# Three of the first six loads issued from ScalarE's DMA queue, in a fused retention and feed-forward kernel

## The chip, the cores and the metric

The kernel runs on one core of one Trainium2 chip. The metric is device time in microseconds of one execution; lower is better. A profile is one further view of a single execution, so its span is compared with that execution's own time.

## The reference

Eight batches of eight heads, 576 positions of 64 values each, go through a retention layer: the scores are weighted with a decay that depends on the distance of the positions, and set to zero above the diagonal. The result, 4608 rows of 512, goes through two matrix products with a tanh Gelu between them.

```python
scores = scale * np.matmul(q, k.transpose(0, 1, 3, 2))
gamma = 1.0 - 2.0 ** (-5.0 - np.arange(H))
rel = pos[:, None] - pos[None, :]
Dmat = np.where(rel >= 0, gamma[:, None, None] ** rel[None, :, :], 0.0)
ret = np.matmul(scores * Dmat[None], v)
x = ret.transpose(0, 2, 1, 3).reshape(B * S, H * D)
h = x @ w_in        
g = 0.5 * h * (1.0 + np.tanh(c * (h + 0.044715 * h * h * h)))
out = g @ w_out
```

## The kernel before

**Work and tiles.** A batch of 576 positions is four chunks of 128 and a tail of 64. Loads fetch 256 positions of four heads at once (256 KB, a "ld" tile of 128 x 512 in 32-bit floats), named by batch, half s of the batch, half hh of the heads, and k, q or v. They are cast to 16 bits (cast_qk, cast_v; v is scaled by a table sc of decays), k and q are transposed on TensorE (tr, a bank of PSUM that ScalarE, VectorE or both, marked S2, copy into the tile T), scores are formed (score_mm, L385) and masked (mask_sc, L408). A running state carries what earlier chunks leave (state_mm, scan, put into the tile tbd); values and inter_mm form the output of the layer, and evac (L534) scales it by the table gx into the rows of x.

The feed-forward part works on a Block of 512 rows: sixteen products up (L583), each followed by a Gelu on ScalarE (L587), then seven products down (L726, called my, mz, mw, mv, mu, my2, mz2), which are a fast matrix multiplication with seven instead of eight products; VectorE and GpSimd form its sums (mix_sa, mix_sc, mix_d). In the last two blocks, the tails of all batches and batch 7, three pairs of the upward products are also done by a saving scheme: pair_a (L615) makes three PSUM banks pv, pw and py, pair_q (L627) lets ScalarE copy pv into cp and VectorE form four sums and differences in q, pair_b adds to py, pair_s adds py to two of the four, and pair_g is the Gelu.

**What sets the order.** Nothing is reordered by a scheduler: each engine runs its instructions in the order in which the program text calls them. The body is a list of units (upward and downward products) with a plan, a hand-written list of steps that follow each unit. The first ten units are empty; their steps are batch 0. Dummy matmuls on a tile of zeros (warm, L138, and pad, L147 and L149, counts in the table pads) keep TensorE running in the first 20 us. They are plain instructions, executed whether TensorE would have had to wait or not.

**Loads.** All loads are issued by SyncE, in the order of the calls of load_qkv and load_w (L188, L272). The first six are k, q for heads 0 to 3 of half 0 of batch 0, k for heads 4 to 7, v for heads 0 to 3, q for heads 4 to 7, and k for heads 0 to 3 of half 1. Eight completion semaphores go round for all loads, so the ninth load issued waits for the first to have landed, and so on; later loads also wait for their buffer.

**The start of ScalarE.** ScalarE begins with a dummy Exp (L88), by which the table of Exp is loaded while other constants are made; then four Exps that make gx (L121), one for sc (L122), one for gt (L124, used by scan), and a dummy Gelu (L125), which brings in the other table for the rest of the kernel. In the plan the first steps on batch 0 are: GpSimd zeroes tbd (L132) and casts q, then k; TensorE transposes q, which ScalarE copies, then k, of which ScalarE copies two quarters and VectorE the others; VectorE's copy waits for ScalarE's; then come the scores of the first four heads, VectorE's cast of the second k, the two masks, the cast of the second q, and so on.

Of the kernel before, what the change touches and what calls it, by code (L numbers as in the profile page):

```python
# [10 lines left out]
AF = mybir.ActivationFunctionType  # L11
ALU = mybir.AluOpType
F32 = mybir.dt.float32
# [6 lines left out]
def kernel(  # L20
# [22 lines left out]
    nc = tc.nc  # L43
# [4 lines left out]
    HP = H // 2  # L48
# [36 lines left out]

    wz = const.tile([128, 256], F16, name="wz")
    nc.vector.memset(wz, 0.0)
    nc.scalar.activation(out=p2[:, 3:4], in_=wz[:, 0:1], func=AF.Exp)  # L88

    lg = const.tile([128, 13], F32, name="lg")  # L90
    nc.vector.memset(lg[:, 12:13], math.log(scale))
# [7 lines left out]
    for hh in range(2):  # L99
# [4 lines left out]
            op=ALU.mult,  # L104
# [12 lines left out]


    gx = const.tile([128, HP, 2, 64], F32, name="gx")
    for p in range(HP):  # L120
        nc.scalar.activation(out=gx[:, p], in_=gi, func=AF.Exp, bias=lg[:, 12:13], scale=lg[:, 8 + p : 9 + p])  # L121
    nc.scalar.activation(out=sc, in_=ex, func=AF.Exp, bias=0.0, scale=-1.0)  # L122
    gt = const.tile([128, HP], F32, name="gt")
    nc.scalar.activation(out=gt, in_=lg[:, 8:12], func=AF.Exp, bias=0.0, scale=128.0)  # L124
    nc.scalar.activation(out=p2[:, 3:4], in_=wz[:, 0:1], func=AF.Gelu_apprx_tanh)  # L125


    tbd = [const.tile([128, NC, HP, 128], F16, name=f"tbd{i}") for i in range(2)]
# [15 lines left out]
    def pad(key, t, o=0):  # L144
        for _ in range(pads.pop(key, 0)):
            if t.dtype == F16:
                nc.tensor.transpose(t[:, 0:128], wz[:, 0:128], ident)  # L147
            else:
                nc.tensor.matmul(t[:, o : o + 128], wz[:, 0:128], wz[:, 0:128], start=(o == 0), stop=True, skip_group_check=True)  # L149

    NJ = NF // 2
# [33 lines left out]
    def load_qkv(b, s, hh, key, home=None):  # L185
        def one(home):
            t = ld(home)
            nc.sync.dma_start(  # L188
                out=t.rearrange("p (h e) -> p h e", h=4),
                in_=SRC[key][b, 4 * hh : 4 * hh + 4, 256 * s : 256 * s + 256, :].rearrange(  # L190
                    "h (p r) d -> p h (r d)", r=2
                ),
            )
            att[b][key, s, hh] = t

        todo.append((one, home))
        pump()
# [33 lines left out]
    def copy(eng, out, in_):  # L231
        (eng.copy if eng is nc.scalar else eng.tensor_copy)(out=out, in_=in_)  # L232
# [208 lines left out]
            )  # L441
            a["rett", hl] = x

    def state_mm(b, ss):
        a = att[b]
        us = [bank("us") for _ in range(2)]
        pad(("us", b, ss[0]), us[0])
        for n, s in enumerate(ss):
            a["U", s] = us, n
            for p in range(HP):  # L450
                hh, pp = divmod(p, 2)
                if p == 2:
                    pad(("us1", b, ss[0]), us[0], 256)
                o = 256 * n + 64 * p
                for r in range(2):
                    for c in range(2):
                        for hl in range(2):
                            w = slice(256 * r + 128 * pp + 64 * hl, 256 * r + 128 * pp + 64 * hl + 64)
                            nc.tensor.matmul(
                                us[c][half[hl], o : o + 64],  # L460
                                a["kq"][half[c], s, hh, 0, w],
                                a["v"][half[c], s, hh, w],
                                start=(r == 0), stop=(r == 1), skip_group_check=True,
                            )

    def scan(b, n):
        a = att[b]
        s, c = divmod(n, 2)
        us, i = a["U", s]
        uc = us[c][:, 256 * i : 256 * i + 256].rearrange("p (q d) -> p q d", d=64)  # L470
        if n > 0:
            t = sb.tile([128, HP, 64], F32, tag="vs", name="vs", bufs=1)
            nc.vector.tensor_tensor(out=t, in0=uc, in1=a["w", n - 1], op=ALU.add)
            uc = t
        w = sb.tile([128, HP, 64], F32, tag="ws", name="ws", bufs=2)
        nc.vector.tensor_tensor(out=w, in0=uc, in1=gt.unsqueeze(2).to_broadcast([128, HP, 64]), op=ALU.mult)  # L476
        a["w", n] = w

    def put(b, n, eng):
        w = att[b]["w", n]  # L480
        for hl in range(2):
            e = (A, V)[hl] if eng is S2 else eng
            copy(e, tbd[b % 2][half[hl], n, :, half[hl]], w[half[hl]])

    def values(b, s):
        a = att[b]
# [28 lines left out]
    def inter_mm(b, s, c):  # L515
        a = att[b]
        n = 2 * s + c
        if n > 0:
            pad(("in", b, n), a["U", (n - 1) // 2][0][0])
            for p in range(HP):  # L520
                hh, pp = divmod(p, 2)
                nc.tensor.matmul(  # L522
                    a["x", s][c][:, 128 * p : 128 * p + 128],
                    tbd[b % 2][:, n - 1, p, :],
                    a["T"][:, s, hh, 1, pp : pp + 3 : 2, half[c]],
                    start=False, stop=True, skip_group_check=True,
                )
# [32 lines left out]
    class Block:  # L560
# [54 lines left out]
        def pair_a(self, j):  # L615
            self.open()
            pv, pw, py = bank("pv"), bank("pw"), bank("py")
            self.pair[j] = pv, pw, py
            f, w = wf[j], w_in_sb[:, :, 256 * j : 256 * j + 256]
            mm = self.pair_mm  # L620
            mm(j, pv[:, 0:256], lambda c: f[:, 2 + c], lambda c: self.x_half(1, 2 + c), True)
            mm(j, pv[:, 256:512], lambda c: f[:, 4 + c], lambda c: self.x_half(0, c))
            mm(j, pw[:, 0:256], lambda c: f[:, c], lambda c: self.xf[2][:, c], True)
            mm(j, py[:, 0:256], lambda c: w[:, c, 0:128], lambda c: self.xf[0][:, c], True)
            mm(j, py[:, 256:512], lambda c: w[:, 2 + c, 128:256], lambda c: self.xf[1][:, c])

        def pair_q(self, j):  # L627
            pv, pw, py = self.pair[j]
            cp = sb.tile([128, 512], F32, tag="cv", name="cp", bufs=2)
            q = sb.tile([128, 1024], F32, tag="T", name="q", bufs=4)  # L630
            self.pair[j] = py, q
            nc.scalar.copy(out=cp, in_=pv)
            c2 = cp.rearrange("p (k c) -> p k c", k=2)
            q4 = q.rearrange("p (m c) -> p m c", m=4)
            nc.vector.tensor_tensor(
                out=q4[:, 0:4:3], in0=py.rearrange("p (k c) -> p k c", k=2), in1=c2, op=ALU.add
            )
            for m, k in ((2, 0), (1, 1)):
                nc.vector.tensor_tensor(out=q4[:, m], in0=pw[:, 0:256], in1=c2[:, k], op=ALU.subtract)

        def pair_b(self, j):
            py, q = self.pair[j]
# [3 lines left out]

        def pair_s(self, j):
            py, q = self.pair[j]
            q4 = q.rearrange("p (m c) -> p m c", m=4)
            nc.vector.tensor_tensor(  # L650
                out=q4[:, 1:3], in0=py.rearrange("p (k c) -> p k c", k=2), in1=q4[:, 1:3], op=ALU.add
            )

        def pair_g(self, j):
            q = self.pair.pop(j)[1]
            nc.scalar.activation(  # L656
                out=self.g(j).rearrange("p h (s c) -> p s h c", s=2),
                in_=q.rearrange("p (s h c) -> p s h c", s=2, h=2),
                func=AF.Gelu_apprx_tanh,
            )  # L660

# [43 lines left out]
        def product(self, m, js=range(NJ), us=(0, 1)):  # L705
# [14 lines left out]
                else:  # L720
                    self.bank[m] = bank(m)
            t = self.bank[m]
            for u in us:
                o = t[u] if isinstance(t, list) else t[:, 256 * u : 256 * u + 256]
                for j in js:
                    nc.tensor.matmul(  # L726
                        o,
                        lhs(j, slice(128 * u, 128 * u + 128)),
                        w_out_sb[:, j, w],
                        start=((u == 0 or isinstance(t, list)) and j == 0 and not more),  # L730
                        stop=(j == NJ - 1), skip_group_check=True,
                    )

        def quad(self, s, k):
            return self.ost[:, :, s, 256 * k : 256 * k + 256]
# [58 lines left out]
                in_=self.ost[:, us[0] : us[0] + n, s, 256 * k : 256 * k + 256],  # L794
            )

        def last(self):
            for m in MS[:-1]:
                self.down(m)
                for q in {"mv": [(0, 1)], "mu": [(1, 0)], "my2": [(1, 1)]}.get(m, ()):  # L800
                    self.store_quad(*q)
            for u in range(2):
                self.product("mz2", us=(u,))
                self.settle("mz2", u)
                self.store_quad(0, 0, (u,), (nc.scalar, nc.sync)[u])
# [26 lines left out]
    def add(plan, *entries):  # L832
        for u, step in entries:
            plan.setdefault(u, []).append(step)
        return plan

    tiles(0)
    E = loan("T", 8, 4)
    E3 = E[:]
# [7 lines left out]
    load_qkv(0, 0, 0, "v", None)  # L847
    load_qkv(0, 0, 1, "q", None)
    load_qkv(0, 1, 0, "k", None)
    load_qkv(0, 0, 1, "v", None)  # L850
    load_qkv(0, 1, 1, "k", None)
    load_qkv(0, 1, 0, "q", None)
# [633 lines left out]
```

## Time and profile before

| what | value |
|---|---|
| median of 4 runs | 298.05 us (297.25 to 298.76) |
| the profiled execution's own time | 297.66 us |
| its span in the profile | 295.9 us |
| granted TensorE clock, share of full | 0.999 |
| TensorE busy in the span | 289.1 us |
| VectorE, ScalarE, GpSimd busy | 230.7, 161.9, 120.9 us |
| bytes moved, mean rate | 52.48 MB, 177 GB/s |

Times in the trace count from the start of the span. A row of the timeline has the start, the duration from the first to the last of the merged instructions, the engine, the line, the operation, output and inputs, the count, and in brackets the idle time of the engine just before, with what ended it. SPq and ACTq are the queues of SyncE and ScalarE in which DMAs are issued: the duration there is that of the issuing, not of the transfer. A row of the view of waits has who waited for whom, the sum in us, how many times, and the longest.

### The profile page before, as it was taken

Reading aid. Unit: us, or ns where it says so; the run is one execution under the profiler, and the core shown is the slowest. Engines: PE = TensorE matmul, PEld = TensorE weight load, DVE = VectorE, ACT = ScalarE, POOL = GpSimd, SP = SyncE. Lnnn points to the kernel's source line nnn. Section 1 sums busy time; section 2 is a strip of 40 time slices with the busy share of each in tenths; the row PEclk is TensorE's granted clock in tenths of the full one; section 3 lists DMA queues with packets and bytes.
Section 4 is the critical chain, followed back from the end, with each engine's and each line's share of the span. In section 5 each row is a group of like instructions: output and inputs, shape, how many; then the busy total and the mean of one; then the engine's idle time right before and its main releaser. Section 6 shows DMA issues by size and latency. Waiting matters only on the chain.

```text
span 295.9 us, 8910 instructions
## 1 busy us (share of the span) xinstructions
PE 289.1 (98%) x3748; PEld 209.0 (71%) x3748; DVE 230.7 (78%) x434; ACT 161.9 (55%) x316; POOL 120.9 (41%) x142
## 2 busy tenths in 40 slices
PE   8989999999999999999999999999999999999995
PEld 6866478888885568656875587558755886786584
DVE  2796899999997997897568756877688198886753
ACT  7338789875546781665446544654345217606720
POOL 6734784375240441282073206369003005711760
PEclk9999999999999999999999999999999999999999
DMA  7999999869879999969983998481120003002204
GB/s 203 304 351 332 310 383 322 233 174 232 212 211 230 326 217 215 300 218 145 273 279 91 136 268 272 111 149 15 66 80 0 2 25 121 0 2 71 71 3 142
DMA packets 94712, 52.48 MB, mean 177 GB/s; under 512 B 38352, under 2 KB 88528, under 8 KB 94672
## 3 DMA queue, kind: packets, MB, share of 16 engines
q1 hardware_dynamic: 94336, 51.26, 65.1%
q10 hardware_dynamic: 336, 0.66, 0.8%
q8 instruction: 29, 0.48, 0.7%
q14 instruction: 11, 0.09, 0.1%
HBM read 36.70 MB, written 9.44 MB: 156 GB/s over the span
## 4 chain that ended last, share of the span: by engine, by line
PE 80%; DMA 9%; SPq 4%; DVE 2%; ACT 1%; POOL 1%; issue 1%; DVEq 0%
PE hp L583 28%; PE my L726 11%; PE mz L726 11%; PE mu L726 5%; PE mw L726 5%; PE mv L726 5%; DMA ld<-in_moe_w_in_dram 4%; PE hp L669 3%; SPq L188 3%; PE xs L495 2%; PE xs L522 2%; DMA ld<-in_moe_w_out_dram 2%; DMA loan<-in_moe_w_in_dram 2%; PE py L613 2%; PE st L395 1%; DMA loan<-in_moe_w_out_dram 1%
## 5 line engine op out<-in xcount | busy, mean ns | idle before, releaser
L583 PE MATMUL hp<-x,w_in_sb 128*128 128x512 f16 x408 | 93.9, 379 | 0.0
L587 ACT ACTIVATE gT<-hp 128x512 f16<-128x512 f32 x112 | 65.8, 598 | 42.2 <-PE hp L583 40.5
L583 PEld LDWEIGHTS <-w_in_sb 128*128 128x128 f16 x448 | 42.5, 98 | 44.4 <-issue 0.3
L726 PEld LDWEIGHTS <-gT 128*128 128x128 f16 x576 | 55.8, 98 | 8.0
L232 POOL CAST kq<-ld 128x512 f16<-128x512 f32 x31 | 21.7, 708 | 54.5 <-DMA ld<-in_k_dram 40.1
L408 DVE TENSOR_TENSOR ret<-st,cm 128x512 f16<-128x512 f32 x64 | 39.9, 679 | 4.0 <-PE st L395 3.7
L241 POOL TENSOR_TENSOR cv<-ld,sc 128x512 f16<-128x512 f32 x28 | 31.2, 1126 | 27.1 <-DMA ld<-in_v_dram 22.7
L232 ACT CAST tbd<-ws 64x256 f16<-64x256 f32 x61 | 24.6, 403 | 23.2 <-DVE ws L476 22.6
L726 PE MATMUL my<-w_out_sb,gT 128*128 128x256 f16 x288 | 34.4, 273 | 0.0
L726 PE MATMUL mz<-w_out_sb,gT 128*128 128x256 f16 x288 | 34.4, 273 | 0.0
L726 PEld LDWEIGHTS <-gsum 128*128 128x128 f16 x288 | 28.0, 98 | 3.4
L698 DVE TENSOR_TENSOR gT<-gT 128x1024 f16<-128x1024 f16 x30 | 29.3, 984 | 0.2
L694 DVE TENSOR_TENSOR gsum<-gT 128x1024 f16<-128x1024 f16 x32 | 24.4, 764 | 2.7 <-ACT gT L656 2.7
L535 DVE TENSOR_TENSOR x<-xs,gx 128x512 f16<-128x512 f32 x32 | 21.5, 682 | 5.6 <-PE xs L522 5.4
L686 DVE TENSOR_TENSOR gdia<-gT 128x512 f16<-128x512 f16 (+1 forms) x30 | 21.6, 722 | 4.0 <-ACT gT L587 2.8
L753 DVE TENSOR_TENSOR ost<-ost,mv 128x512 f32<-128x512 f32 x18 | 11.5, 682 | 15.2 <-issue 10.3
L694 POOL TENSOR_TENSOR gsum<-gT 128x1024 f16<-128x1024 f16 x4 | 8.9, 2224 | 34.8 <-ACT gT L656 31.8
L669 PE MATMUL hp<-x,w_in_sb 128*128 128x256 f16 x160 | 19.0, 273 | 0.9 <-DVE x L535 0.9
L669 PEld LDWEIGHTS <-w_in_sb 128*128 128x128 f16 x160 | 15.3, 98 | 3.0 <-issue 1.2
L726 PE MATMUL mu<-w_out_sb,gsum 128*128 128x256 f16 x144 | 17.2, 273 | 0.1
L726 PE MATMUL mw<-w_out_sb,gdia 128*128 128x256 f16 x144 | 17.2, 273 | 0.0
L726 PE MATMUL mv<-w_out_sb,gsum 128*128 128x256 f16 x144 | 17.2, 273 | 0.0
(114 smaller groups left out, 403.5 us busy)
## 6 DMA issues: line engine op xcount, KB each, us to landing
ld<-in_k_dram SPq DMA_DIRECT2D x30, 256.0 KB, 5.2
ld<-in_q_dram SPq DMA_DIRECT2D x30, 256.0 KB, 5.2
ld<-in_v_dram SPq DMA_DIRECT2D x30, 256.0 KB, 5.6
out_dram<-ost SPq DMA_DIRECT2D x14, 512.0 KB, 4.6
loan<-in_moe_w_out_dram SPq DMA_DIRECT2D x12, 256.0 KB, 5.3
loan<-in_moe_w_in_dram SPq DMA_DIRECT2D x8, 256.0 KB, 6.1
ld<-in_moe_w_in_dram SPq DMA_DIRECT2D x8, 256.0 KB, 6.1
ld<-in_moe_w_out_dram SPq DMA_DIRECT2D x4, 256.0 KB, 5.4
```

The source lines that it names most:

```text
L232: (eng.copy if eng is nc.scalar else eng.tensor_copy)(out=out, in_=in_)
L241: eng.tensor_tensor(out=unperm(att[b]["v"][:, s, hh, :]), in0=perm(t), in1=sc[:, 8 * hh : 8 * hh + 8] .rearrange("p (r h) -> p r h", r=2) ...
L408: nc.vector.tensor_tensor(out=x.rearrange("p (a m) -> p a m", a=2), in0=st[hl].rearrange("p (a m) -> p a m", a=2), in1=cm.rearrange("p r s ...
L535: nc.vector.tensor_tensor(out=xb[b][:, :, 2 * s + c].rearrange("p s q i -> p q s i"), in0=att[b]["x", s][c].rearrange("p (q s i) -> p q s ...
L583: nc.tensor.matmul(hp, w_in_sb[:, ct, 128 * f : 128 * f + 128], x[:, :, ct, :], start=(ct == 0), stop=(ct == 3),)
L587: nc.scalar.activation(out=self.g(f // 2)[:, f % 2], in_=hp, func=AF.Gelu_apprx_tanh)
L669: nc.tensor.matmul(hp[:, 256 * h : 256 * h + 256], w_in_sb[:, ct, 256 * j + 128 * h : 256 * j + 128 * h + 128], xb[self.b][:, :, 2 * u : 2 ...
L686: e.tensor_tensor(out=self.sa[:, j : j + n], in0=g[:, :, 0, 0:256], in1=g[:, :, 1, 256:512], op=ALU.add)
L694: e.tensor_tensor(out=self.sc[:, j : j + n], in0=g[:, :, 0], in1=g[:, :, 1], op=ALU.add)
L698: e.tensor_tensor(out=g.rearrange("p j h c -> p j (h c)")[:, :, 256:768].rearrange("p j (h c) -> p j h c", h=2), in0=g[:, :, :, 0:256], in ...
L726: nc.tensor.matmul(o, lhs(j, slice(128 * u, 128 * u + 128)), w_out_sb[:, j, w], start=((u == 0 or isinstance(t, list)) and j == 0 and not ...
L753: nc.vector.tensor_tensor(out=out, in0=in0, in1=t, op=op)
```

## The change

The dummy Exp, the six activations that make the tables and the dummy Gelu become a function exps(), which is called after the sixth call of load_qkv. The loads of q and v for heads 0 to 3 of half 0, and of k for heads 0 to 3 of half 1, are issued by ScalarE, the others by SyncE as before. As exps() comes after them in the program, ScalarE's queue holds the three issues first, then the table load and the activations.

Further edits lie in the same diff. In pair_a the two products that fill the halves of pv change places. In pair_q the tile cp is gone: ScalarE copies pv into the middle of q, and one subtraction over both halves replaces two; pair_s and pair_g change only in how they name q. In product, the order of the sixteen matmuls of my is by j first and then by u; before, all eight j came for u = 0 and then for u = 1. state_mm, scan and put get an argument by which they can treat half of the heads (with new names state_h, scan_h and put_h that nothing calls), and last() an argument plan that no call gives. The dummy counts and the plan are the same.

```diff
-    nc.scalar.activation(out=p2[:, 3:4], in_=wz[:, 0:1], func=AF.Exp)
...
-    for p in range(HP):
-        nc.scalar.activation(out=gx[:, p], in_=gi, func=AF.Exp, bias=lg[:, 12:13], scale=lg[:, 8 + p : 9 + p])
-    nc.scalar.activation(out=sc, in_=ex, func=AF.Exp, bias=0.0, scale=-1.0)
     gt = const.tile([128, HP], F32, name="gt")
-    nc.scalar.activation(out=gt, in_=lg[:, 8:12], func=AF.Exp, bias=0.0, scale=128.0)
-    nc.scalar.activation(out=p2[:, 3:4], in_=wz[:, 0:1], func=AF.Gelu_apprx_tanh)
+
+    def exps():
+        nc.scalar.activation(out=p2[:, 3:4], in_=wz[:, 0:1], func=AF.Exp)
+        for p in range(HP):
+            nc.scalar.activation(out=gx[:, p], in_=gi, func=AF.Exp, bias=lg[:, 12:13], scale=lg[:, 8 + p : 9 + p])
+        nc.scalar.activation(out=sc, in_=ex, func=AF.Exp, bias=0.0, scale=-1.0)
+        nc.scalar.activation(out=gt, in_=lg[:, 8:12], func=AF.Exp, bias=0.0, scale=128.0)
+        nc.scalar.activation(out=p2[:, 3:4], in_=wz[:, 0:1], func=AF.Gelu_apprx_tanh)
...
-            nc.sync.dma_start(
+            (nc.scalar if (b, key, s, hh) in AQ else nc.sync).dma_start(
...
-            mm(j, pv[:, 0:256], lambda c: f[:, 2 + c], lambda c: self.x_half(1, 2 + c), True)
-            mm(j, pv[:, 256:512], lambda c: f[:, 4 + c], lambda c: self.x_half(0, c))
+            mm(j, pv[:, 0:256], lambda c: f[:, 4 + c], lambda c: self.x_half(0, c), True)
+            mm(j, pv[:, 256:512], lambda c: f[:, 2 + c], lambda c: self.x_half(1, 2 + c))
...
-            nc.scalar.copy(out=cp, in_=pv)
...
+            nc.scalar.copy(out=q[:, 1:3], in_=pv.rearrange("p (k c) -> p k c", k=2))
             nc.vector.tensor_tensor(
-                out=q4[:, 0:4:3], in0=py.rearrange("p (k c) -> p k c", k=2), in1=c2, op=ALU.add
+                out=q[:, 0:4:3], in0=py.rearrange("p (k c) -> p k c", k=2), in1=q[:, 2:0:-1], op=ALU.add
             )
-            for m, k in ((2, 0), (1, 1)):
-                nc.vector.tensor_tensor(out=q4[:, m], in0=pw[:, 0:256], in1=c2[:, k], op=ALU.subtract)
+            nc.vector.tensor_tensor(
+                out=q[:, 1:3],
+                in0=pw[:, 0:256].unsqueeze(1).to_broadcast([128, 2, 256]),
+                in1=q[:, 1:3],
+                op=ALU.subtract,
+            )
...
-            for u in us:
-                o = t[u] if isinstance(t, list) else t[:, 256 * u : 256 * u + 256]
-                for j in js:
...
+            order = [(u, j) for j in js for u in us] if m == "my" else [(u, j) for u in us for j in js]
+            for u, j in order:
...
+    AQ = {(0, "q", 0, 0), (0, "v", 0, 0), (0, "k", 1, 0)}
     tiles(0)
...
     load_qkv(0, 1, 0, "k", None)
+    exps()
     load_qkv(0, 0, 1, "v", None)
```

More of the change, by code (lines that the diff above doesn't have):

```diff
@@ L442, in mask_tail, with state_h, state_mm @@
             a["rett", hl] = x
-    def state_mm(b, ss):
+    def state_h(b, s, hh):
+        state_mm(b, [s], (hh,))
+    def state_mm(b, ss, hhs=(0, 1)):
         a = att[b]
         us = [bank("us") for _ in range(2)]
-        pad(("us", b, ss[0]), us[0])
+        pad(("us", b, ss[0]) if len(hhs) == 2 else ("us", b, ss[0], hhs[0]), us[0])
         for n, s in enumerate(ss):
-            a["U", s] = us, n
-            for p in range(HP):
+            for hh in hhs:
+                a["U", s, hh] = us, n
+            for p in range(2 * hhs[0], 2 * hhs[-1] + 2):
                 hh, pp = divmod(p, 2)
@@ L464, in state_mm, with scan, scan_h, put @@
                             )
-    def scan(b, n):
+    def scan(b, n, hhs=(0, 1)):
         a = att[b]
         s, c = divmod(n, 2)
-        us, i = a["U", s]
-        uc = us[c][:, 256 * i : 256 * i + 256].rearrange("p (q d) -> p q d", d=64)
+        us, i = a["U", s, hhs[0]]
+        qs = slice(2 * hhs[0], 2 * hhs[-1] + 2)
+        nq = qs.stop - qs.start
+        uc = us[c][:, 256 * i : 256 * i + 256].rearrange("p (q d) -> p q d", d=64)[:, qs]
         if n > 0:
-            t = sb.tile([128, HP, 64], F32, tag="vs", name="vs", bufs=1)
-            nc.vector.tensor_tensor(out=t, in0=uc, in1=a["w", n - 1], op=ALU.add)
+            t = sb.tile([128, HP, 64], F32, tag="vs", name="vs", bufs=1)[:, qs]
+            nc.vector.tensor_tensor(out=t, in0=uc, in1=a["w", n - 1][:, qs], op=ALU.add)
             uc = t
[L475 to L479, printed above, removed]
+        if ("w", n) not in a:
+            a["w", n] = sb.tile([128, HP, 64], F32, tag="ws", name="ws", bufs=2)
+        nc.vector.tensor_tensor(
+            out=a["w", n][:, qs], in0=uc, in1=gt[:, qs].unsqueeze(2).to_broadcast([128, nq, 64]), op=ALU.mult
+        )
+    def scan_h(b, n, hh):
+        scan(b, n, (hh,))
+    def put(b, n, eng, hhs=(0, 1)):
         w = att[b]["w", n]
+        qs = slice(2 * hhs[0], 2 * hhs[-1] + 2)
         for hl in range(2):
             e = (A, V)[hl] if eng is S2 else eng
-            copy(e, tbd[b % 2][half[hl], n, :, half[hl]], w[half[hl]])
+            copy(e, tbd[b % 2][half[hl], n, qs, half[hl]], w[half[hl], qs])
+    def put_h(b, n, hh, eng):
+        put(b, n, eng, (hh,))
     def values(b, s):
@@ L518, in inter_mm @@
         if n > 0:
-            pad(("in", b, n), a["U", (n - 1) // 2][0][0])
+            pad(("in", b, n), a["U", (n - 1) // 2, 0][0][0])
             for p in range(HP):
@@ L628, in pair_q @@
             pv, pw, py = self.pair[j]
-            cp = sb.tile([128, 512], F32, tag="cv", name="cp", bufs=2)
-            q = sb.tile([128, 1024], F32, tag="T", name="q", bufs=4)
+            q = sb.tile([128, 4, 256], F32, tag="T", name="q", bufs=4)
             self.pair[j] = py, q
-            nc.scalar.copy(out=cp, in_=pv)
-            c2 = cp.rearrange("p (k c) -> p k c", k=2)
-            q4 = q.rearrange("p (m c) -> p m c", m=4)
+            nc.scalar.copy(out=q[:, 1:3], in_=pv.rearrange("p (k c) -> p k c", k=2))
             nc.vector.tensor_tensor(
-                out=q4[:, 0:4:3], in0=py.rearrange("p (k c) -> p k c", k=2), in1=c2, op=ALU.add
+                out=q[:, 0:4:3], in0=py.rearrange("p (k c) -> p k c", k=2), in1=q[:, 2:0:-1], op=ALU.add
             )
-            for m, k in ((2, 0), (1, 1)):
-                nc.vector.tensor_tensor(out=q4[:, m], in0=pw[:, 0:256], in1=c2[:, k], op=ALU.subtract)
+            nc.vector.tensor_tensor(
+                out=q[:, 1:3],
+                in0=pw[:, 0:256].unsqueeze(1).to_broadcast([128, 2, 256]),
+                in1=q[:, 1:3],
+                op=ALU.subtract,
+            )
         def pair_b(self, j):
@@ L648, in pair_s @@
             py, q = self.pair[j]
-            q4 = q.rearrange("p (m c) -> p m c", m=4)
             nc.vector.tensor_tensor(
-                out=q4[:, 1:3], in0=py.rearrange("p (k c) -> p k c", k=2), in1=q4[:, 1:3], op=ALU.add
+                out=q[:, 1:3], in0=py.rearrange("p (k c) -> p k c", k=2), in1=q[:, 1:3], op=ALU.add
             )
@@ L657, in pair_g @@
                 out=self.g(j).rearrange("p h (s c) -> p s h c", s=2),
-                in_=q.rearrange("p (s h c) -> p s h c", s=2, h=2),
+                in_=q.rearrange("p (s h) c -> p s h c", s=2),
                 func=AF.Gelu_apprx_tanh,
@@ L722, in product @@
             t = self.bank[m]
-            for u in us:
-                o = t[u] if isinstance(t, list) else t[:, 256 * u : 256 * u + 256]
-                for j in js:
[L726 to L732, printed above, removed]
+            order = [(u, j) for j in js for u in us] if m == "my" else [(u, j) for u in us for j in js]
+            for u, j in order:
+                nc.tensor.matmul(
+                    t[u] if isinstance(t, list) else t[:, 256 * u : 256 * u + 256],
+                    lhs(j, slice(128 * u, 128 * u + 128)),
+                    w_out_sb[:, j, w],
+                    start=((u == 0 or isinstance(t, list)) and j == 0 and not more),
+                    stop=(j == NJ - 1), skip_group_check=True,
+                )
         def quad(self, s, k):
@@ L795, in store_quad, with last @@
             )
-        def last(self):
-            for m in MS[:-1]:
+        def last(self, plan={}):
+            for i, m in enumerate(MS[:-1]):
                 self.down(m)
@@ L801, in last @@
                     self.store_quad(*q)
+                for step in plan.get(i, ()):
+                    step()
             for u in range(2):
```

## The prediction

> **What bounds the kernel now.** I read the page first, for the engine that is full:
>
> ```profile
> PE 289.1 (98%) x3748; PEld 209.0 (71%) x3748; DVE 230.7 (78%) x434; ACT 161.9 (55%) x316; POOL 120.9 (41%) x142
> ...
> PE   8989999999999999999999999999999999999995
> ```
>
> TensorE is busy for 289.1 of 295.9 us, so nearly every microsecond is TensorE's own. Which idle stretches are left? The view of waits, for TensorE alone, names all that end on another engine:
>
> ```profile
> PE warm L138 <- DVE wz L87: 1.1, 1, 1.1
> PE hp L669 <- DVE x L535: 0.9, 1, 0.9
> PE tr L342 <- ACT kq L232: 0.5, 1, 0.5
> PE st L395 <- DVE T L232: 0.2, 1, 0.2
> PE tr L352 <- DVE vs L473: 0.2, 1, 0.2
> ```
>
> By the timeline the first four are the start and 22.56, 15.69 and 14.65 us; after 22.56 us TensorE runs almost without a gap to 292.3 us. So a late TensorE at 23 us stays late to the end, and an early one would end early. The chain of waits goes through DMA until 45 us, but TensorE beside it is full from 24 us on: that chain is not what I price. The change sits in the first 10 us, so next the timeline of that stretch:
>
> ```profile
> 0.73 1.28 ACT L88 ACT_TABLE_LOAD   x1 [0.73 <-PEq L1470]
> 0.73 0.45 SPq L188 DMA_DIRECT2D ld<-in_k_dram  x1
> ...
> 1.24 0.49 SPq L188 DMA_DIRECT2D ld<-in_q_dram  x1
> ...
> 1.79 0.50 SPq L188 DMA_DIRECT2D ld<-in_k_dram  x1
> ...
> 4.05 1.66 SPq L188 DMA_DIRECT2D ld<-in_v_dram  x1
> ...
> 4.64 1.17 POOL L232 CAST kq<-ld 128x512 f16<-128x512 f32 x2 [0.25 <-DMA ld<-in_q_dram]
> 5.28 0.20 ACT L125 ACTIVATE p<-wz 128x1 f32<-128x1 f16 x1
> ...
> 5.74 0.99 ACT L232 COPY T<-tr 128x512 f16<-128x512 f16 x2 [0.26 <-PE tr L342]
> ...
> 6.16 0.83 PE L149 MATMUL st<-wz 128*128 128x128 f16 x12
> ...
> 6.76 0.29 DVE L232 COPY T<-tr 128x256 f16<-128x256 f16 x1 [3.77 <-ACT T L232]
> ...
> 6.92 0.55 PE L395 MATMUL st<-T 64*64 64x128 f16 x16
> ...
> 7.40 1.51 PE L147 MATMUL tr<-ident,wz 128*128 128x128 f16 x24
> 7.51 1.29 DVE L408 TENSOR_TENSOR ret<-st,cm 128x512 f16<-128x512 f32 x2
> ```
>
> The reader is to see four things. ScalarE is never free before 5.48 us: table, exps, second table, dummy Gelu follow each other without a gap. Its first useful work, the copy of the first transposes, then waits only 0.26 us for TensorE. VectorE's half of that copy waits for ScalarE (3.77 us), and the first scores start at 6.92 us, just when the dummy matmuls ahead of them run out and 0.1 us before VectorE's half is there: no slack. Behind the scores stand 24 more dummies (1.51 us) that run whether needed or not, so TensorE keeps any delay.
>
> **What the Trainium skill says.** DMA: Bandwidth & Descriptors, section Issuing engines are not separate DMA queues: transfers from SyncE and ScalarE run on the same 16 engines, and a second issuer saves only sequencer time. The trace agrees as far as it goes: in stretches of half a microsecond the DMA share is 1.10 at 2.5 us, never under 0.89 from there to 10 us, with one issuer alone; there is hardly bandwidth left to win. The same page, section Queues, rings and completion order: SyncE and ScalarE each own a row of rings, one ring per DMA engine. No stretch of this trace has both issuing at once, so it doesn't show this. ScalarE: Activation LUTs, section What ACT_TABLE_LOAD costs: a load of 1283 ns and a drain of about 1380. The trace has 1.28 us for both loads, but the next ACTIVATE starts right behind (2.02 us), so no drain is paid here. TensorE: Matmul & The Clock Gate, section What's actually happening: the clock halves after an idle window of about 3.4 us. Between 20 and 24 us TensorE is busy 2.94 us of 4 and the granted clock stays 1.00.
>
> **The change part by part.** 1. *Three issues put ahead of the exps on ScalarE.* The built program has q, v and k first, then the table load. The three issues on SyncE at 0.73, 1.24 and 1.79 us took 0.45, 0.49 and 0.50 us, the next would start at 2.33: 1.60 us. ScalarE's own issues of stores near the end took 1.80 us for four, 0.45 each, so 1.35 to 1.60. I take 1.60, as these loads have the same shape as SyncE's. Everything on ScalarE follows in order: first table at 2.33, exps until 5.6, dummy Gelu 6.88, ready for the first copy at about 6.99 (neighbours overlap 0.09).
>
> 2. *What of that reaches TensorE.* The two copies, 0.58 and 0.36 us, ended at 6.73 because the second waited for the second transpose. Now both transposes are done, so they run back to back: 0.58 + 0.36 - 0.09 = 0.85, end 7.84; VectorE's half starts 7.86 where it was 6.76. **Shift 1.10 us**: of 1.60, the idle 0.26, the wait between the copies 0.14 and the overlap 0.09 are taken up. With issues at 0.45 it is 0.85. VectorE's next operations (key cast, two masks 1.29 us, query cast) stand behind this copy, TensorE's scores and 24 dummies too.
>
> 3. *Is it taken up later?* Only a wait on something that does not move could do so. VectorE waits 0.5 us at 10.8 for scores, then runs with about 1.0 us idle from 12 to 22 us (busy 9.02 of 10), and of that 0.53 us is for a ScalarE copy that follows VectorE's own results. The TensorE waits at 14.65, 15.69 and 22.56 end on this chain. I count nothing taken up: the 1.10 us reaches 23 us, and stays.
>
> 4. *Three issues taken from SyncE.* The seventh load was issued at 4.05 and held to 5.71. It can now be issued near 2.33. But bytes, not issues, set the landings: measured from start of issue, the first nine landed at 3.7, 4.5, 6.5, 7.4, 8.3, 9.1, 10.1, 10.9 and 11.7 us, mostly 0.85 us apart (256 KB at 300 GB/s). Two rings alternate, so q and k land together near 4.5 and the sixth near 9.1; the cast of the second query, 8.71 before, moves to 9.8, so that holds. The query cast on GpSimd could at best start at 4.39, when its zeroing ends: 0.25 us sooner, worthless while ScalarE is busy until 6.9. GpSimd's waits of 1.74 and 1.56 us for v may shrink; the state product at 11.24 used the second, but its other partner is 1.1 us later anyway. Gain 0; with ScalarE free it would be at most 0.25.
>
> 5. *Exps later.* sc is needed at 7.54 by GpSimd and comes at 5.5 (3.87 before); gt at 12.04, gx at 14.5. Cost 0 under those covers.
>
> 6. *The pair forms.* Per pair VectorE has one subtraction of 512 columns (at most 0.69, the row of that size) for two that took 0.74 together, and a new wait on itself for the result read before: its rows overlap by 0.08. Net between -0.05 and +0.1 for six pairs, beside a TensorE without a gap from 241 to 292 us: 0. Its cover gone, at most 0.6. ScalarE's copy now waits for the large buffer, last read long before. The swapped pv products cost the same; some waits of TensorE on itself are new, but such waits stand in the same blocks now and the rows stay at 0.216 us per 512 columns: between -0.1 and +0.3, taken 0.
>
> 7. *Order of my.* The last Gelu is needed seven matmuls later. TensorE hides it already: 1.94 us at 280.03 against 1.91 elsewhere, so gain at most 0.03. The same 16 matmuls. The half-head helpers are never called, their defaults give the old program.
>
> Sum: +1.10. The profiled execution took 297.66 (295.9 span, 1.76 around it), so 298.76; it lies 0.39 under the median of 298.05, on which the forecast stands: **299.15 us**, +0.37%.
>
> **Rivals.** *ScalarE's third issue is held back.* SyncE's seventh (1.66 us) and eighth (0.69) show that issuing stops at about five unlanded loads. If that limit is common to both issuers, the sixth load, ScalarE's or SyncE's third, waits for the first landing, 3.7 us, instead of ending at 2.29: 1.4 to 1.6 more, +2.6: 300.65. For it: nothing here shows two issuers; against: separate rings by the skill. *The delay is taken up* (the other side: not slower). If the waits at 14.65, 15.69 and 22.56 (0.17 + 0.46 + 0.92 = 1.55 us) end on loads and casts that keep their times, such as the w_in casts at 13.38 and 21.65, they shrink by the 1.10: 298.05; it decides once at least 1.10 of the 1.55 is of that kind. Against it is the busy VectorE of step 3. *The clock falls*: a gap of 1.1 us about 7 us would have to fill a window. One window of 3.4 us at half clock adds up to 1.7: 300.85. Against: 20 to 24 us. *No effect of the issuer*, if the table were loaded ahead of the issues, is excluded: the built order has it behind.
>
> **How the numbers follow.** Forecast 0.60, held issue 0.20, taken up 0.12, clock 0.04, a gain not seen here 0.04. The forecast's own range is 298.7 (short issues, some wait shrinking) to 299.6 (pair waits, longer issues). The range of 8 in 10 goes from 298.0, with the case taken up, to 300.7, with the held issue. A measurement of this kernel can tell about 0.5% from no change, 1.49 us: 296.56 to 299.54. Faster 0.04; same 0.62 (forecast mostly, and taken up); slower 0.34 (held issue, clock, and a sixth of the forecast).
>
> **What would show it.** Right: ScalarE's table load at 2.3 us, first copy near 7.0, VectorE's half near 7.9, a TensorE wait of about 1 us at 7, the hp wait about 1.1 us later, at 23.7. Held issue: one ScalarE issue over 1 us long and the copy near 8.5. Taken up: hp at 22.6 as before. Wrong altogether if the first copy starts before 6.5 us, or if TensorE shows new gaps after 24 us.

## The result and the profile after

The changed kernel took 299.84 us (median of 39 runs, 298.42 to 301.40) beside 298.42 us for the kernel before (60 runs, 297.25 to 300.33). The ratio is 1.0045, with a 95% interval of 1.0035 to 1.0055: **1.34 us slower** by the ratio (the two medians lie 1.42 us apart), within the half per cent that the prediction calls no change, and clear of zero. Forecast was +1.10 us (+0.37%).

The profiled execution of the changed kernel took 299.83 us with a span of 298.0, like its median. The one of before (297.66) lies 0.76 us under the median of its 60 runs, so times of the one trace set against the other overstate the loss by about that much. The page after, engines and slices:

```profile
PE 290.3 (97%) x3748; PEld 209.9 (70%) x3748; DVE 231.0 (78%) x428; ACT 162.3 (54%) x316; POOL 120.7 (41%) x142
...
PE   8998998999999999999999999999999999999995
PEclk9999999999999999999999999999999999999999
```

TensorE is as full as before, and the clock is whole in every slice (0.998 as mean). So the loss is in short waits again. The view of waits after, TensorE alone (who waited for whom, sum, times, longest):

```profile
PE warm L140 <- DVE wz L87: 1.1, 1, 1.1
PE hp L686 <- DVE x L552: 0.8, 1, 0.8
PE xs L512 <- DVE ret L410: 0.7, 2, 0.4
PE tr L344 <- ACT kq L234: 0.4, 1, 0.4
PE st L397 <- DVE T L234: 0.6, 1, 0.6
PE st L397 <- ACT T L234: 0.2, 1, 0.2
PE tr L354 <- DVE vs L481: 0.2, 1, 0.2
```

Two rows are new or longer: the 0.7 us for VectorE's masked scores (ret) and the 0.6 for T. By the timeline the waits for ret lie at 37.22 and 49.52 us and the one for T at 45.18, after the point where the prediction had the story end. First its own stretch, the timeline of the start after:

```profile
0.73 0.49 ACTq L190 DMA_DIRECT2D ld<-in_q_dram  x1
...
1.25 0.58 ACTq L190 DMA_DIRECT2D ld<-in_v_dram  x1
...
1.86 0.53 ACTq L190 DMA_DIRECT2D ld<-in_k_dram  x1
...
2.42 1.28 ACT L122 ACT_TABLE_LOAD   x1 [2.42 <-issue]
...
4.86 1.17 POOL L234 CAST kq<-ld 128x512 f16<-128x512 f32 x2 [0.47 <-DMA ld<-in_q_dram]
...
6.76 1.04 POOL L243 TENSOR_TENSOR cv<-ld,sc 128x512 f16<-128x512 f32 x1 [0.73 <-DMA ld<-in_v_dram]
...
7.08 0.84 ACT L234 COPY T<-tr 128x512 f16<-128x512 f16 x2
7.96 0.29 DVE L234 COPY T<-tr 128x256 f16<-128x256 f16 x1 [4.97 <-ACT T L234]
7.98 0.69 PE L397 MATMUL st<-T 64*64 64x128 f16 x16 [0.20 <-ACT T L234]
```

The three issues took about half a microsecond each and none was held back. The table load follows at 2.42 us, the first copy at 7.08, VectorE's half at 7.96 (6.76 before), the scores at 7.98 (6.92 before). The rows of GpSimd (POOL) show a thing that the prediction held possible and gave no weight: v comes earlier. GpSimd scaled the first v at 7.54 before and at 6.76 now, the second at 10.14 and 9.39. The chain that ended last, which went through DMA at the start before, now goes through ScalarE:

```profile
0.73 0.49 ACTq L190
1.25 0.58 ACTq L190
1.86 0.53 ACTq L190
...
7.18 0.76 ACT T L234 x2
7.96 0.30 DVE T L234
...
22.95 0.70 DVE x L552
23.65 0.04 issue
23.69 2.78 PE hp L686 x24
```

The hp matmuls that stood at 22.56 us stand at 23.69: +1.13, where 1.10 was forecast. Up to here the prediction holds. Beyond it some of VectorE's sums of two 16-bit tiles take longer than before. The timeline of before from 32 to 40 us, VectorE (DVE) and GpSimd:

```profile
32.05 1.09 DVE L698 TENSOR_TENSOR gT<-gT 128x1024 f16<-128x1024 f16 x1
33.06 2.47 DVE L408 TENSOR_TENSOR ret<-st,cm 128x512 f16<-128x512 f32 x4
...
33.58 1.04 POOL L241 TENSOR_TENSOR cv<-ld,sc 128x512 f16<-128x512 f32 x1
...
38.64 3.56 POOL L331 TENSOR_TENSOR w_out_sb<-ld 128x256 f16<-128x256 f32 x3 [1.37 <-DMA ld<-in_moe_w_out_dram]
38.66 0.68 DVE L694 TENSOR_TENSOR gsum<-gT 128x1024 f16<-128x1024 f16 x1
39.26 2.35 DVE L241 TENSOR_TENSOR cv<-loan,sc 128x512 f16<-128x512 f32 x2
```

And after (L715 was L698, L711 was L694):

```profile
33.02 1.21 POOL L243 TENSOR_TENSOR cv<-ld,sc 128x512 f16<-128x512 f32 x1
33.25 1.53 DVE L715 TENSOR_TENSOR gT<-gT 128x1024 f16<-128x1024 f16 x1
34.70 2.47 DVE L410 TENSOR_TENSOR ret<-st,cm 128x512 f16<-128x512 f32 x4
...
39.47 1.60 POOL L333 TENSOR_TENSOR w_out_sb<-ld 128x256 f16<-128x256 f32 x2 [0.58 <-DMA ld<-in_moe_w_out_dram]
...
40.41 1.21 DVE L711 TENSOR_TENSOR gsum<-gT 128x1024 f16<-128x1024 f16 x1
```

Before, VectorE's masks at 33.06 were under way when GpSimd began cv, and gsum took its bare 0.68 us; there it was GpSimd's sum of w_out, begun at 38.64, that lengthened (1.29 us, where the one at 36.55 had taken 0.72), though the two rows begin 0.02 us apart. After, GpSimd begins cv 0.56 us earlier, since the w_in casts ahead of it, which wait for a load, begin at 30.87 instead of 31.19 and take less time; VectorE comes 1.2 later. Now GpSimd is ahead at both places. VectorE's sum ends at 33.25 + 1.53 = 34.78, which is 0.55 us after GpSimd's end (33.02 + 1.21 = 34.23); gsum ends at 41.62, again 0.55 after GpSimd's end at 41.07. It reads as an operation that could not start until the other was done. The Trainium skill, SBUF — State Buffer, section Who interferes with whom, says as much: a VectorE instruction with two inputs in SBUF and a GpSimd instruction that reads SBUF use one port, and whichever issues first holds it for its whole length. The trace agrees at these two places; the page gives no price, here it is 0.44 us (1.53 against 1.09, which is itself more than the 0.68 of such a sum alone) and 0.53. Call this a meeting. The kernel before has meetings too, its 1.09 us among them; the change adds to them at these places. The masks, at 33.06 before, are 1.64 us later after, the next pair of scaled v 2.28.

So there were two theories for the 1.34 us. **Late ScalarE** (theory A in the expectations): the first copy comes late, and that delay alone stays to the end, as forecast. **Meetings** (theory P, the theory of VectorE and GpSimd): the delay is only part of it; since the loads come earlier and VectorE later, GpSimd gets ahead of VectorE and blocks it.

### The profile page after: what moved, and what is told of

Read it like the earlier page. It is cut to its first block, busy times and chain, and to the rows that moved or that the text cites. A ratio compares the mean times of both kernels' runs of the same rounds, so it can differ in the third digit from the quotient of the medians.

```text
span 298.0 us, 8903 instructions
## 1 busy us (share of the span) xinstructions
PE 290.3 (97%) x3748; PEld 209.9 (70%) x3748; DVE 231.0 (78%) x428; ACT 162.3 (54%) x316; POOL 120.7 (41%) x142
## 4 chain that ended last, share of the span: by engine, by line
PE 87%; ACT 4%; DMA 4%; DVE 2%; issue 1%; ACTq 1%; SPq 0%
PE hp L600 31%; PE mz L742 11%; PE my L742 11%; PE mu L742 5%; PE mw L742 5%; PE mv L742 5%; PE hp L686 4%; DMA loan<-in_moe_w_out_dram 4%; PE xs L512 3%; PE st L397 2%; PE xs L539 2%; PE py L630 2%; PE us L465 1%; PE tr L344 1%; ACT tbd L234 1%; DVE ret L410 1%
## 5 line engine op out<-in xcount | busy, mean ns | idle before, releaser
L243 POOL TENSOR_TENSOR cv<-ld,sc 128x512 f16<-128x512 f32 x28 | 32.5, 1174 | 31.1 <-DMA ld<-in_v_dram 25.0
L234 POOL CAST kq<-ld 128x512 f16<-128x512 f32 x31 | 20.7, 678 | 55.7 <-DMA ld<-in_k_dram 42.1
L715 DVE TENSOR_TENSOR gT<-gT 128x1024 f16<-128x1024 f16 x30 | 29.3, 982 | 0.2
L711 DVE TENSOR_TENSOR gsum<-gT 128x1024 f16<-128x1024 f16 x32 | 24.9, 779 | 2.7 <-ACT gT L673 2.7
L703 DVE TENSOR_TENSOR gdia<-gT 128x512 f16<-128x512 f16 (+1 forms) x30 | 21.0, 702 | 4.5 <-ACT gT L604 2.8
L711 POOL TENSOR_TENSOR gsum<-gT 128x1024 f16<-128x1024 f16 x4 | 8.9, 2226 | 34.8 <-ACT gT L673 31.8
```

Of the source, the lines that this page charges most:

```text
L243: eng.tensor_tensor(out=unperm(att[b]["v"][:, s, hh, :]), in0=perm(t), in1=sc[:, 8 * hh : 8 * hh + 8] .rearrange("p (r h) -> p r h", r=2) ...
L703: e.tensor_tensor(out=self.sa[:, j : j + n], in0=g[:, :, 0, 0:256], in1=g[:, :, 1, 256:512], op=ALU.add)
L711: e.tensor_tensor(out=self.sc[:, j : j + n], in0=g[:, :, 0], in1=g[:, :, 1], op=ALU.add)
L715: e.tensor_tensor(out=g.rearrange("p j h c -> p j (h c)")[:, :, 256:768].rearrange("p j (h c) -> p j h c", h=2), in0=g[:, :, :, 0:256], in ...
```

## The experiments

A ratio is to the kernel before, timed again together with each group of runs, with its 95% interval. Microseconds worked out from a ratio take its distance from 1 times about 298.5 us. None of these kernels leaves out work, except that fewer_dummies leaves out dummies.

**The change split in two.** head_only is the kernel before with the change's loads and exps() alone; rest_only is the changed kernel with all loads on SyncE and exps() ahead of them.

```diff
-    AQ = {(0, "q", 0, 0), (0, "v", 0, 0), (0, "k", 1, 0)}
+    AQ = set()
+    exps()
...
-    exps()
```

> The kernel before with the loads' part of the change alone: three loads from ScalarE, the exps behind them; pair forms, order of my and everything else as before. Theory A (the cost is ScalarE's late first copy): all of the change's time, 298.4 + 1.3 = 299.7 us, first copy at 7.1 us. Rival B (the pair forms or the order of my cost it): 298.4 to 298.7.

> The changed kernel with all loads on SyncE and the exps ahead of them, so that ScalarE's and SyncE's orders at the start are those of before; pair forms and order of my as changed. Theory A: no difference from before, within 0.3 us, first copy at 5.7 us. Rival B: 299.4 to 299.8.

Measured: head_only 1.0058 (1.0041 to 1.0075), rest_only 0.9997 (0.9982 to 1.0012). The loss is all in the loads' part (head_only's median, 300.3 us, lies even above the 299.7 expected); the pair forms and the order of my cost nothing that can be seen.

**The delay alone.** late_scalar is the kernel before with the four exps of gx done twice: ScalarE is late, no load moves.

```diff
-    for p in range(HP):
+    for p in [*range(HP), *range(HP)]:
```

> The kernel before with the four exps that make gx done twice: 1.63 us more of ScalarE ahead of its first copy, no load moved. Theory A: as the change, first copy near 7.1 us and 1.1 to 1.4 us slower, 299.5 to 299.8. Rival C (the cost comes from loads that land in another order or at other times): no more than 0.3 us slower, since no load moves.

Measured: 1.0021 (1.0007 to 1.0036), 0.63 us: between what the two theories had expected. Its first copy is at 6.92 us and its hp at 23.59, +1.03 beside the change's +1.13. Nearly the same delay at 23 us costs about half of what the change costs; its interval lies below head_only's, timed with it, and just reaches that of the change. VectorE's two sums have their lengths of before, since GpSimd came later too (its cv at 34.74 us, its sum of w_out at 40.11):

```profile
33.21 1.09 DVE L698 TENSOR_TENSOR gT<-gT 128x1024 f16<-128x1024 f16 x1
...
39.82 0.68 DVE L694 TENSOR_TENSOR gsum<-gT 128x1024 f16<-128x1024 f16 x1
```

**The loads alone.** table_first is the changed kernel with a dummy Exp on ScalarE ahead of its three issues, so that the table is loaded first.

```diff
+    nc.scalar.activation(out=p2[:, 3:4], in_=wz[:, 0:1], func=AF.Exp)
...
     def exps():
-        nc.scalar.activation(out=p2[:, 3:4], in_=wz[:, 0:1], func=AF.Exp)
```

> The changed kernel with the dummy Exp, and so the first table load, ahead of ScalarE's three issues; the other activations stay behind them. The table load occupies the engine while its queue issues, so the exps start near 2.4 us and not 3.8. Theory A: the first copy is late by about 0.3 us, of which the 0.26 us of idle time takes most: within 0.3 us of before. Rival C: as slow as the change, 299.7, since the loads go as in the change. Rival D (moving loads to a second issuer helps once ScalarE is not late): under 298.1.

Measured: 1.0002 (0.9985 to 1.0019). The timeline of its start shows why: ScalarE's queue issues while the table is still being loaded.

```profile
0.73 1.28 ACT L121 ACT_TABLE_LOAD   x1 [0.73 <-PEq L1491]
...
1.04 0.51 ACTq L191 DMA_DIRECT2D ld<-in_q_dram  x1
1.58 0.52 ACTq L191 DMA_DIRECT2D ld<-in_v_dram  x1
...
2.13 0.53 ACTq L191 DMA_DIRECT2D ld<-in_k_dram  x1
...
6.28 0.99 ACT L235 COPY T<-tr 128x512 f16<-128x512 f16 x2
```

The first copy is at 6.28, 0.54 us later than before, and hp at 22.75, 0.19 later: most of this delay is gone by then. Moving the three issues without the late copy neither gains nor costs. The loads do not land as in the change, though: the first v lands at 7.94 us, against 6.61 in the change and 7.40 before.

**A smaller delay.** one_load leaves only q on ScalarE.

```diff
-    AQ = {(0, "q", 0, 0), (0, "v", 0, 0), (0, "k", 1, 0)}
+    AQ = {(0, "q", 0, 0)}
```

> The changed kernel with the first q alone issued by ScalarE, exps behind it. Theory A: ScalarE is 0.5 us late, which its idle 0.26 us and the wait between its two copies take up: first copy near 6.0 us, time within 0.3 us of before. A cost in proportion to the number of issues would give 0.45 us over before.

Measured: 1.0004 (0.9983 to 1.0025); first copy 6.13, hp 22.82. Only one issue's time stands ahead of the table load, and nothing is left of it at the end.

**The first copies on VectorE.** vector_copies has VectorE copy the first two transposes, with the loads as in the change.

```diff
-        (0, L(tr, 0, 0, 0, 1, A)),
+        (0, L(tr, 0, 0, 0, 1, V)),
...
-        (0, L(tr, 0, 0, 0, 0, S2)),
+        (0, L(tr, 0, 0, 0, 0, V)),
```

> The changed kernel, but VectorE instead of ScalarE copies the first two transposes; ScalarE's three issues and its exps as changed. Theory A (the cost starts with ScalarE's late first copy): VectorE is idle there, the copies take 0.42 us each behind their transposes, first scores near 7.2 us, time within 0.3 us of before. If the cost were in the issues or the order of the loads themselves: as the change, 1.3 us over before.

Measured: 1.0015 (0.9996 to 1.0035): 0.45 us by the ratio, not the 0.3 at most that was expected, and not to be told from before; by its ratio faster than the change, whose interval it touches. Here the loads land as in the change (the first v at 6.59). The scores came at 7.70, against 7.98 in the change and 6.92 before: q's cast begins at 4.83, 0.19 later than before, and the dummies and transposes behind it take longer in this execution, so that the second transpose is ready only after 7 us. hp was at 22.96, and gsum took 0.68 us.

**The dummies.** fewer_dummies has 7 dummy matmuls behind the first scores, where the change has 24.

```diff
-        ("tr", 0, 0, 1, 0): 24,
+        ("tr", 0, 0, 1, 0): 7,
```

> The changed kernel with 7 instead of 24 dummy matmuls behind the first scores. If the dummies are what keeps TensorE late, as the prediction had it: 17 times 0.063 = 1.07 us less, 298.8. If VectorE keeps it, whose two masks and query cast stand behind the late scores: no gain, 299.8, and TensorE waits where the dummies were.

Measured: 1.0044 (1.0027 to 1.0061); nothing gained. Its timeline behind the first scores:

```profile
8.60 0.56 PE L149 MATMUL tr<-ident,wz 128*128 128x128 f16 x7
8.71 1.29 DVE L410 TENSOR_TENSOR ret<-st,cm 128x512 f16<-128x512 f32 x2
...
9.80 1.04 POOL L243 TENSOR_TENSOR cv<-ld,sc 128x512 f16<-128x512 f32 x1 [1.61 <-DMA ld<-in_v_dram]
9.92 1.21 DVE L234 CAST kq<-ld 128x512 f16<-128x512 f32 x1
...
11.18 0.40 PE L344 MATMUL tr<-ident,kq 128*128 128x128 f16 x4 [1.29 <-DVE kq L234]
```

TensorE saves 17 dummies and then waits 1.29 us for the cast of the second query, which stands behind the two masks on VectorE. The cast begins at 9.92 us with or without the dummies, so without them VectorE keeps the delay. The cast takes 1.21 us where it took 0.42 before; GpSimd began cv 0.12 us ahead of it. The change has this meeting too (0.81 us, at the same 9.92), and so have all the kernels here that keep the change's loads and late copies: it isn't what tells them apart.

**Loads later.** extra_load is the changed kernel with one redundant load of 256 KB (into a buffer that a later load overwrites) behind the fourteenth, so that all that follow come later. It moves more bytes, not less.

```diff
+    nc.sync.dma_start(out=E2[3], in_=moe_w_in[0:128, 0:512])
```

> The changed kernel with one load of 256 KB more, into a buffer that is written over before use, ahead of the first feed-forward weights, so that all later loads land about 0.85 us later. Theory P (part of the cost is that GpSimd, which follows the loads, now runs ahead of VectorE and the two hold each other up between 30 and 50 us): 0.4 to 0.9 us faster than the change, 298.9 to 299.4 where the change has 299.8. Theory A alone (a delay on ScalarE, loads do not matter): no faster than the change, 299.8 to 300.6.

Measured: 1.0019 (1.0002 to 1.0036): more work, and by the ratios about 0.8 us less than the change, whose interval it just reaches. GpSimd is behind again at both places in its timeline, and VectorE's sums have their lengths of before:

```profile
33.23 1.09 DVE L715 TENSOR_TENSOR gT<-gT 128x1024 f16<-128x1024 f16 x1
...
34.76 1.04 POOL L243 TENSOR_TENSOR cv<-ld,sc 128x512 f16<-128x512 f32 x1
...
39.85 0.68 DVE L711 TENSOR_TENSOR gsum<-gT 128x1024 f16<-128x1024 f16 x1
40.25 0.87 POOL L333 TENSOR_TENSOR w_out_sb<-ld 128x256 f16<-128x256 f32 x1 [1.95 <-DMA ld<-in_moe_w_out_dram]
```

**GpSimd later, loads as they are.** This takes the meetings away without touching a load or ScalarE: small memsets of the dummies' tile of zeros, no longer read by then, ahead of GpSimd's cv (four) and of its two sums of w_out (six). gpsimd_later_first has the four only; before_gpsimd_later is the kernel before with all ten.

```diff
+    def idle(n):
+        for _ in range(n):
+            nc.gpsimd.memset(wz, 0.0)
...
+        (21, L(idle, 4)),
         (21, L(cast_v, 1, 0, 1, G)),
...
+        (31, L(idle, 6)),
         (31, L(mix_w_out, 1, "sums", G)),
```

> The change, with ten small memsets of a tile of zeros added on GpSimd (about 0.26 us each by the 128x512 memset of 0.52): four just ahead of its second scaled v of batch 1 (33.02 us in the changed kernel) and six ahead of the two sums of w_out at 39.47. No load, no copy of ScalarE and no instruction of VectorE is touched; GpSimd only does more. Theory that GpSimd and VectorE hold each other up: VectorE's 1024-column sums at 33.25 (1.53 us) and 40.41 (1.21 us) go back to 0.7 to 1.1 and 0.68, the masks near 34.7 start by 34.3, the scaled v near 41.54 by 40.6, and the time falls by 0.4 to 0.8 us from the changed kernel's, to 299.1 to 299.5 (+0.2 to +0.35 % of before). Theory that the late ScalarE copy alone costs the whole: no gain, or a loss by the added work, 299.8 or more (+0.45 %).

> As the run before it, with the first four memsets only. By the theory of VectorE and GpSimd the first long sum (1.53 us at 33.25) shortens by 0.4 to 0.8 us, the second stays long or meets GpSimd at another place: a time between the changed kernel and the run with both, near 299.5. By the other theory 299.8 or more.

> Control: the kernel before with the same ten memsets in the same places. By the theory of VectorE and GpSimd the two engines do not meet at these places in the kernel before, beyond the 1.09 us sum at 32.05, so there is little to win: between -0.1 and +0.3 us. If the memsets were good for something else, it would gain the 0.4 to 0.8 us here too.

Measured: gpsimd_later 1.0005 (0.9991 to 1.0019), 298.90 us; the first four alone 1.0038 (1.0022 to 1.0053), 299.36 us; the control 1.0029 (1.0011 to 1.0047). Ten added instructions take away nearly the whole loss, and cost 0.86 us in the kernel before (there TensorE waits 0.9 us for GpSimd's cv). That is more than the meetings' theory had expected of either. The first four alone can't be told from the change. The timeline of gpsimd_later (L719 and L715 are VectorE's two sums):

```profile
32.24 1.42 POOL L139 MEMSET wz<- 128x256 f16 x4
...
33.42 0.68 DVE L719 TENSOR_TENSOR gT<-gT 128x1024 f16<-128x1024 f16 x1
33.62 1.39 POOL L247 TENSOR_TENSOR cv<-ld,sc 128x512 f16<-128x512 f32 x1
34.07 2.61 DVE L414 TENSOR_TENSOR ret<-st,cm 128x512 f16<-128x512 f32 x4
...
38.72 2.15 POOL L139 MEMSET wz<- 128x256 f16 x6
...
39.96 0.68 DVE L715 TENSOR_TENSOR gsum<-gT 128x1024 f16<-128x1024 f16 x1
```

Now VectorE is ahead at 33.42, its sum takes 0.68 us, and GpSimd's cv is the one that lengthens (1.39, alone 1.04). So this run takes away more than the change had added: the kernel before has 1.09 us here. The six memsets stand beside gsum and don't hold it, in line with the skill's section, which exempts a GpSimd instruction that only writes.

All the kernels, from their timelines and runs (us). The columns hp and my give the start of the hp products that stood at 22.56 us before, and of the first downward product:

| kernel | first ScalarE copy | hp | gsum near 40: start, length | my | ratio |
|---|---|---|---|---|---|
| before | 5.74 | 22.56 | 38.66, 0.68 | 56.65 | 1 |
| rest_only | 5.75 | 22.83 | 39.07, 0.68 | 57.51 | 0.9997 |
| table_first | 6.28 | 22.75 | 38.85, 0.68 | 57.24 | 1.0002 |
| one_load | 6.13 | 22.82 | 39.02, 0.69 | 56.95 | 1.0004 |
| vector_copies | (VectorE) | 22.96 | 39.07, 0.68 | 56.77 | 1.0015 |
| before_gpsimd_later | 5.99 | 22.84 | 40.21, 0.68 | 57.85 | 1.0029 |
| late_scalar | 6.92 | 23.59 | 39.82, 0.68 | 58.10 | 1.0021 |
| extra_load | 7.09 | 23.74 | 39.85, 0.68 | 58.07 | 1.0019 |
| gpsimd_later | 7.09 | 23.96 | 39.96, 0.68 | 57.98 | 1.0005 |
| gpsimd_later_first | 7.08 | 23.96 | 39.97, 1.22 | 58.41 | 1.0038 |
| fewer_dummies | 7.09 | 23.98 | 40.52, 1.22 | 58.92 | 1.0044 |
| head_only | 7.09 | 23.70 | 40.20, 1.22 | 58.61 | 1.0058 |
| after | 7.08 | 23.69 | 40.41, 1.21 | 59.12 | 1.0045 |

The column hp has two groups, on time and a microsecond late. The late group splits again, by the length of gsum: 0.68 us goes with ratios up to 1.0021, 1.2 us with 1.0038 and more. The control, on time at hp, is late only behind its own memsets. None of these kernels beats the one before.

## Why the prediction was right in its number and half right in its reasons

**Step 1, right.** Three issues took 0.49, 0.58 and 0.53 us; the table load moved by 1.69 us (forecast 1.60), the first copy came at 7.08 (6.99).

**Step 2, right in time, wrong in one reason.** VectorE's half came at 7.96 (7.86), and hp was +1.13 (+1.10). TensorE's wait behind ScalarE was 0.20 us and not about 1: in this execution the dummies before it took longer (the first eleven behind warm 1.38 us, 0.99 before), while head_only, with the same start of ScalarE, waits 0.84. That the "24 more dummies" are why TensorE keeps any delay fell with fewer_dummies: without them VectorE's masks and cast keep it.

**Step 3, wrong: "I count nothing taken up: the 1.10 us reaches 23 us, and stays."** It reaches 23 us; it doesn't stay in full. Without the meetings that the change adds, about the same delay costs 0.63 us (late_scalar), 0.57 (extra_load) or 0.15 (gpsimd_later, at most 0.57 by its interval). The rival that it is taken up was thus partly right, but not at the waits it named: those end at 23 us. By the traces hardly anything is taken up before my either: in the three profiles of late kernels without the meeting at 40 us (late_scalar, extra_load, gpsimd_later) my stands at 58.05 us as a mean, 0.96 after the mean of the four kernels on time at the head of the table. Behind 90 us the distance of each TensorE product from the same one before stays the same within 0.07 us in every trace. Between my and 90 us it changes by -0.3 to +1.8 us from one profile to another, more than the half microsecond that is sought. So if the delay is taken up, it is there, and by what isn't shown.

**Step 4, right that nothing is gained, wrong that nothing is lost.** q landed 0.2 us later than before (4.81 against 4.59) and the sixth load at 8.63 (9.1 expected), but v about 0.75 earlier, and GpSimd, which follows the loads, with it. The step looked only at who waits for these loads, and not at what runs beside GpSimd when it moves. With VectorE late, GpSimd is first at 33 and 40 us. Of the 1.34 us this makes 1.34 - 0.63 = 0.71 by late_scalar and 0.77 by extra_load, about half. By gpsimd_later it is 1.34 - 0.15 = 1.19, but that is too much, since this run also takes away a meeting which the kernel before has. So the meetings are about half of the loss or more; the intervals do not allow a closer figure, and how much each of the two costs isn't shown.

**Steps 5 to 7, right**: rest_only is at 0.9997, and late exps made nobody wait but ScalarE's own copy. Of the rivals, the held issue (ScalarE's longest is 0.58 us) and the clock (0.998 as mean) did not come about.

**The sum.** 1.10 us was forecast and 1.34 came, because two errors nearly cancel: about 0.5 us too much was kept in step 3 (0.95 by gpsimd_later), and about 0.7 us of step 4 was missed (1.2 by gpsimd_later). That the number came out is in part luck. The prediction's own mark for "wrong altogether", new gaps of TensorE after 24 us, did appear. The origin, ScalarE's late first copy, is shown: where it comes only 0.54 or 0.39 us late (table_first, one_load) no loss is seen. That meetings of VectorE and GpSimd make a good part of the loss is shown by making the same delay without them (late_scalar) and by taking them away in two ways, with later loads and with a later GpSimd. The last is the clearest by its interval, but it moves GpSimd everywhere behind the memsets, and not at these two places alone.

## What to carry to other kernels

An engine's first useful work decides what may stand ahead of it: here half a microsecond per issued load, less the engine's idle time, went straight into its first copy, and a table load could go first, since the issues then ran beside it. When an edit moves one of VectorE and GpSimd against the other, compare the rows of their two-input operations side by side far behind the edit: a sum that has grown from 0.7 to 1.2 or 1.5 us, ending half a microsecond after a row of GpSimd, has very likely been waiting for it. And a forecast that comes out right should still be split into its parts, since here two wrong terms made a good sum.

## What the runs showed of the hardware that was not expected

- ScalarE's queue issues loads while ScalarE loads a table: issues at 1.04 and 1.58 us beside a table load from 0.73 to 2.01 (table_first). In the other order the table load waits for the issues (2.42 us in the change).
- Two issuers side by side held neither back: ScalarE's took 0.49, 0.58 and 0.53 us while SyncE issued its own. The Trainium skill, DMA: Bandwidth & Descriptors, section Queues, rings and completion order, gives each its own rings; this case now shows both queues issuing together, though not the rings.
- More work can be faster: ten memsets on GpSimd (3.57 us of its time) brought the ratio from the change's 1.0045 to 1.0005, one more load of 256 KB to 1.0019.
